# Part of the output projection made inside attention's last steps, and the first row pairs normalized two pairs later

## The chip, the cores and the metric

The kernel runs on one core of a Trainium2 chip. The metric is device time in microseconds, the median of several runs; one further execution was profiled. Engines are named as in the profile: PE (TensorE, PEld its weight loads), ACT (ScalarE), DVE (VectorE), POOL (GpSimd), SP (SyncE, which issues DMAs).

## What is computed

Four residual sublayers over x of 2048 rows and 640 columns, in float32: attention with 32 heads of 20 dimensions, then a Fourier mixing, and both again.

```python
x = x + _A_ref(_layernorm(x), A_wqkv, A_wo)        # softmax attention, o @ wo at its end
x = x + _B_ref(_layernorm(x), dft_seq..., dft_hid...)   # Real(DFT_seq(DFT_hidden(x)))
x = x + _A_ref(_layernorm(x), A_wqkv, A_wo)
x = x + _B_ref(_layernorm(x), dft_seq..., dft_hid...)
```

## The kernel before

The kernel makes two layers, each of attention and Fourier, with the same code. Matrix products other than scores and values are done with each operand split into a high and a low part (`split`, three matmuls for each product: `three`). Nothing is scheduled by a planner: the order of a Python program is the order of each engine's queue, and each engine takes its queue strictly in order.

**Attention.** `sweep` goes through 512 steps (8 groups of four heads, 4 blocks of 512 query columns, 16 blocks of 128 keys `kc`). A step n has two halves of scores, `scores(n, 0)` and `scores(n, 1)`, each two matmuls into one PSUM tile `psc` and one exp on ACT over 128 x 1024 into a tile `e`; and later `values(n)`, four matmuls of 32 columns from those two e tiles into `acc` (eight matmul records each). The tiles go round in rings:

```python
p = bank(f"p{(2 * n + j) % 3}", [128, 2, 512], "psc")
e = s.e[n, j] = s.room(f"e{(2 * n + j) % 7}", [2, 512], F32, "e")
```

so a score waits until the exp three halves back has read its tile, and an exp waits until the values that read its tile, seven halves back, are done. The values lag the scores: without filling work, a round of the loop is "s s v", where v is that of two steps before. At the end of 16 key blocks `finish` (DVE) normalizes `acc` and POOL stores the result to DRAM in 16 DMAs (`o`).

The order in a step can be written out by hand: `plan(n)` may return a string for several steps, with "s" a half of scores, "v" the values of the next owed step, "f" a call of `block` (work for PE from elsewhere) and "n" a call of `fill`. It does so in the earlier part of attention, where the rest of the QKV projection is made; there the strings are "sssfsssvvssvv" and "ssfsssvvsssvvsssfssvvsssnvv". In the last 90 steps or so there is no such work left, and the order is "ssv" throughout. In those steps DVE checks the Fourier matrices (tile `cq`), splits the weights `wo` and `wh`, and SP loads them, from a list that `done()` returns; one item of it is taken at every second step (`tasks`), not in steps 54 to 63 of 64.

**Projection** (class `Project`). The 2048 rows are 16 row tiles n, in 8 pairs p; the result of a pair is added to the pair's x (tile `xr`, four in rotation) by `product(n)`: for each half of 320 columns, 5 chunks of 128 dimensions by three matmuls, 15 in all, into one of four PSUM banks in rotation, and one DVE instruction that adds it to x with the row sums. The operand `o` comes by `fetch(k, m)` from DRAM, in tiles of two row tiles, four in rotation; two are fetched in the last steps of attention (`early`), two at the start of the projection, the others after pairs 1 and 3. After each pair:

- `normal(p - 1)`, first half: ACT scales (tile `na`), DVE combines (tile `fold`); for pairs 2, 3, 6 and 7 also DVE sums `fold2`, and in its second half ACT and DVE split them into `xn`, which the Fourier part needs;
- `moments(p)`: SP stores x, POOL makes the mean, ACT the sums of squares (`xsq`), POOL the factors (`ars`, `nb`), DVE the sums and differences `g`; for pairs 0 and 2 `edge` (ACT, DVE) handles row 0; for pair 2 DVE waits there for ACT;
- `ahead`: loads or splits parts of the Fourier matrix (tiles `craw`, `chl`).

`mids`, at the start, clears a tile on POOL and splits a few columns on ACT and DVE.

**Fourier** accumulates over the `xn` and `chl` tiles (`pacc`) and then makes the hidden transform (`phid`).

Of the kernel before, what the change touches and what calls it, by code (L numbers as in the profile page):

```python
# [19 lines left out]
ND = D // 128  # L20
# [4 lines left out]
NP = NT // 2  # L25
NQ = NT // 4
LATE = (1, 4, 6)
FIRST = (0, 1, 4, 5)
HD = D // 2
TOL = 2.0 ** -32  # L30
# [5 lines left out]
def mha_fnet_kernel(ctx, tc, x_in, wqk, wv, wo, seq, hid, nat_seq, nat_hid, out):  # L36
# [44 lines left out]
    def split(hl_h, hl_l, src, vector=False):  # L81

        if vector:
            V.tensor_copy(hl_h, src)  # L84
        else:
            A.activation(hl_h, src, AF.Copy)
        V.tensor_tensor(hl_l, src, hl_h.bitcast(F32), op=OP.subtract)  # L87

    def three(out_ap, pairs_h, pairs_l, start, stop):

        (ah, al), (bh, bl) = pairs_h, pairs_l
        PE.matmul(out_ap, ah, bh, start=start, stop=False)  # L92
        PE.matmul(out_ap, ah, bl, start=False, stop=False)  # L93
        PE.matmul(out_ap, al, bh, start=False, stop=stop)  # L94
# [37 lines left out]
    class Qkv:  # L132
# [48 lines left out]
        def fetch(s, c, room=None, tag="wraw", wait=False):  # L181
            s.raw[c] = (room or s.fill)(tag, [ND, 128], F32, "wraw")
            if wait:
                V.memset(s.raw[c][:, 0, 0:1], 0.0)
            nc.sync.dma_start(s.raw[c], wqk[c])
# [268 lines left out]
    class Attention:  # L454
# [156 lines left out]
        def run(s, done, project, check):  # L611

            work, tasks, later = s.a.work(), s.a.vweights(1, s.a.fill, pause=[lambda: None] * 2), list(check)
            s.work, s.blocks, s.after, s.rest, s.more, s.landed = True, 0, None, 0, False, 0


            def due(n):
                return s.blocks < 58 or s.blocks >= 91 or (n - 1) % NT in (2, 7, 12)

            def block(n):  # L620
                try:
                    f = next(work)
                    s.blocks += 1
                    s.more = f is True
                    s.after = (n + (2 if n < s.THIN else 4), f) if f and not s.more else None
                    s.rest = s.after[0] + 2 if s.after else n
                except StopIteration:
                    s.work = False
                    tasks.extend(done())

            def fill(n):
                if s.after:
                    if n >= s.after[0]:
                        f, s.after = s.after[1], None
                        f()
                elif s.work and n >= max(s.rest, s.THIN) and due(n + 1):
                    block(n)
                    s.rest = max(s.rest, n + 2)
                    return s.work and not s.a.silent

            def plan(n):
                if s.blocks >= 58 or s.after:
                    return
                whole = 32 <= s.blocks < 48
                if n % 4 == 1 and n + (4 if whole else 8) < s.THIN and (whole or s.blocks % 2 == 0):
                    return "sssfsssvvssvv" if whole else "ssfsssvvsssvvsssfssvvsssnvv"

            def compare(n):


                if n < 8:
                    return
                for _ in range(2):
                    if not later or n < s.landed or (len(check) - len(later)) * 490 >= n * len(check):
                        break
                    task = later.pop(0)
                    if isinstance(task, tuple):
                        s.landed = n + 5
                        task = task[1]
                    task()  # L660

            def need(n, *keys):
                while not all(k in s.a.made for k in keys):
                    if s.after:
                        fill(s.after[0])
                    else:
                        block(n)

            def begin(n, g, qb, kc):


                if qb == NB - 1 and g + 1 < H // 4:
                    when, to = 0, g + 1
                    c0, c1 = to * 80 // 128, ((to + 1) * 80 - 1) // 128
                    keys = [c0, (c1, 0) if to in LATE else c1, ND + c0, ND + c1] + (["v"] if to >= 4 else [])
                else:
                    when, to, keys = 5, g, [(((g + 1) * 80 - 1) // 128, qb + 1)]
                if to != g or g in LATE and qb < NB - 1:
                    if kc == when:
                        need(n, *keys)  # L680
                        s.shift = s.a.bound(to, s.room)
                    if kc - when in (0, 3, 5):
                        next(s.shift)

                if tasks and n % 2 == 0 and n >= 16 and n % 64 < 54:
                    tasks.pop(0)()
                for f in project.early.get(n, []):
                    f()

            s.sweep("b", begin, fill, plan, block, compare)  # L690
            assert not s.work and not later and not tasks, (len(later), len(tasks))

        def general(s, done, project):

# [231 lines left out]
    class Project:  # L926
        def __init__(s, att, src, dst):
            s.att, s.src, s.dst, s.w, s.raw = att, src, dst, {}, {}
            s.sum = {}
            s.oh, s.x, s.xn, s.rs, s.f, s.g, s.nb = {}, {}, {}, {}, {}, {}, {}  # L930

            s.early = {474: [lambda: s.fetch(0, 0)], 503: [lambda: s.fetch(0, 1)]}

        def weights(s, dc):

# [5 lines left out]
            return load, lambda: split(s.w[dc][:, 0], s.w[dc][:, 1], s.raw[dc], vector=True)  # L941

        def setup(s):
            s.ot = [s.late(f"o{m}", [2, ND, 256], F32R, "o") for m in range(2)]

        def fetch(s, k, m):

            o = s.ot[(2 * k + m) % 4]
            t = 2 * k + m * NP
            nc.sync.dma_start(o.bitcast(F32), s.att.o.rearrange("j (c p) t -> p j c t", p=128)[:, :, :, t * 128:(t + 2) * 128])  # L950
            for i in range(2):
                s.oh[4 * k + 2 * i + m] = o[:, :, :, i * 128:(i + 1) * 128]

        def load(s, p):
            if p < NP:
# [3 lines left out]
        def product(s, n):  # L959
            x = s.x[n // 2][:, n % 2]  # L960
            for i in range(2):
                p = bank(f"b{4 + (2 * n + i) % 4}", [128, 512], "py")[:, :HD]
                cols = slice(i * HD, (i + 1) * HD)
                for dc in range(ND):
                    three(p, [s.oh[n][:, k, dc] for k in range(2)],
                          [s.w[dc][:, k, cols] for k in range(2)], dc == 0, dc == ND - 1)
                V.scalar_tensor_tensor(x[:, cols], p, 1.0, x[:, cols], op0=OP.mult, op1=OP.add,  # L967
                                       accum_out=s.sums(n // 2)[:, i, n % 2:n % 2 + 1])

# [59 lines left out]
                split(xn[:, 0], xn[:, 1], t[k])  # L1029

        def run(s):
            for m in range(2):
                s.ot.append(s.room(f"o{2 + m}", [2, ND, 256], F32R, "o"))
                s.fetch(1, m)
            s.next.mids()
            for p in range(NP):
                if p:
                    s.load(p + 3)
                for n in (2 * p, 2 * p + 1):
                    s.product(n)  # L1040
                if p in (1, 3):
                    for m in range(2):
                        s.fetch(p // 2 + 2, m)

                parts = s.normal(p - 1) if p else iter(())
                next(parts, None)
                s.moments(p)
                list(parts)
                if p == 1:
                    s.next.ahead(0)  # L1050
                elif p in (3, 4, 5):
                    s.next.ahead(p - 2)
            list(s.normal(NP - 1))
# [7 lines left out]
    class Fourier:  # L1061
# [60 lines left out]

        def mids(s):
            x = s.keep("mids", [4, 80], F32R, "mids")
            G.memset(x.bitcast(F32), 0.0)
            s.mid, s.uc = [x[:, 0], x[:, 1]], [x[:, 2], x[:, 3]]
            split(s.mid[0][:, :8], s.mid[1][:, :8], s.midraw.rearrange("p r k i -> p (r k i)"))


        ORDER = (0, 1, 4, 5, 2, 6, 3, 7) + tuple(range(8, 16))  # L1130
# [250 lines left out]
    def layer(start, src, dst, general, tasks, after):  # L1381
# [14 lines left out]
        def done():  # L1396

            fill.close()
            xt.close()
            f.late = Pool(f"late{tag}", "right")  # L1400
            p.late = Pool(f"early{tag}", "right")
            pairs = [p.weights(k) for k in range(ND)] + [f.weights(k) for k in range(6)]
            out = [pairs[0][0]]
            for (_, parts), after in zip(pairs, pairs[1:] + [None]):
                out += [after[0], parts] if after else [parts]
            p.setup()
            out += [lambda: f.edges(0)] + [lambda k=k: p.load(k) for k in range(4)] + [lambda: f.edges(1)]
            return out

        if general:  # L1410
# [138 lines left out]
```

## Time and profile before

| | us |
|---|---|
| median of 3 runs (2474.61 to 2474.91) | 2474.65 |
| profiled execution | 2476.03 |
| its span (first to last instruction) | 2474.0 |
| ACT busy in it, of which exps (L521) | 2116.6, 1917.6 |
| attention's exps of the first layer, from 87.4 to the last one's end at | 1098.8 |
| projection of the first layer (tile py), starts of its matmuls from 1099.9 to | 1171.3 |

The granted clock of PE was 0.999 of full speed. In the timelines a row is: start, duration (from the first start to the last end, where several instructions are merged), engine, line, operation, tiles written <- read, shapes, count, and in brackets the idle time before it with what ended it. In the windows a row is: the window, its length, then for each engine shown its busy time and number of instructions, the granted clock, the DMA share and GB/s. An exp's record begins when ACT takes it up, so that in a gapless row of exps the records overlap. Ends of matmuls are modelled, and a busy PE is not a full one: two or four matmuls on different rows or columns of the array run side by side.

### The profile page before, as it was taken

Reading aid. Unit: us, or ns where it says so; the run is one execution under the profiler, and the core shown is the slowest. Engines: PE = TensorE matmul, PEld = TensorE weight load, DVE = VectorE, ACT = ScalarE, POOL = GpSimd, SP = SyncE. Lnnn points to the kernel's source line nnn. Section 1 sums busy time; section 2 is a strip of 40 time slices with the busy share of each in tenths; the row PEclk is TensorE's granted clock in tenths of the full one; section 3 lists DMA queues with packets and bytes.
Section 4 is the critical chain, followed back from the end, with each engine's and each line's share of the span. In section 5 each row is a group of like instructions: output and inputs, shape, how many; then the busy total and the mean of one; then the engine's idle time right before and its main releaser. Section 6 shows DMA issues by size and latency. Waiting matters only on the chain. (4 is left out here: it accounts for less than half of the span.)

```text
span 2474.0 us, 43743 instructions
## 1 busy us (share of the span) xinstructions
PE 2447.5 (99%) x16350; PEld 1174.9 (47%) x16350; DVE 984.4 (40%) x2174; ACT 2116.6 (86%) x2430; POOL 526.9 (21%) x1034
## 2 busy tenths in 40 slices
PE   8999999999999999999999999999999999999998
PEld 7644444543333332249885444454433333322596
DVE  6244442233343333416763444323333232332275
ACT  6699998899999999975457989888999999999752
POOL 2012211022111212113321212211211212222233
PEclk9999999999999999999999999999999999999999
DMA  5223231223232314427552332312221312233455
GB/s 184 99 88 125 83 110 55 75 69 118 67 100 83 107 62 130 126 86 245 190 182 95 112 100 92 109 53 70 86 77 56 96 59 72 64 97 96 130 204 194
DMA packets 127460, 262.65 MB, mean 106 GB/s; under 512 B 29168, under 2 KB 53520, under 8 KB 127236
## 3 DMA queue, kind: packets, MB, share of 16 engines
q1 hardware_dynamic: 88644, 159.88, 19.6%
q0 software_dynamic: 38592, 99.85, 12.6%
q8 instruction: 132, 2.16, 0.4%
q14 instruction: 92, 0.75, 0.1%
HBM read 175.29 MB, written 84.31 MB: 105 GB/s over the span
## 5 line engine op out<-in xcount | busy, mean ns | idle before, releaser
L521 ACT ACTIVATE e<-psc 128x1024 f32<-128x1024 f32 x2048 | 1917.6, 1120 | 105.6 <-PE psc L518 94.6
L529 PE MATMUL acc<-e,v 128*32 128x512 f32 x8192 | 1041.6, 601 | 0.4 <-DVE of L536 0.3
L518 PE MATMUL psc<-stq,stk 62*128 62x512 f32 x4096 | 765.4, 450 | 2.1 <-ACT e L521 1.1
L518 PEld LDWEIGHTS psc<-stq,stk 62*128 62x128 f32 x4096 | 340.2, 184 | 744.7 <-ACT e L521 623.6
L529 PEld LDWEIGHTS acc<-e,v 128*32 128x32 f32 x8192 | 212.2, 108 | 380.0 <-issue 344.8
L99 PE MATMUL pqk<-xt,wqk 128*128 128x512 f32 x1200 | 319.3, 407 | 0.8 <-DVE xt L87 0.6
L550 POOL DMA_DIRECT2D o<-oh x256 | 132.1, 524 | 821.0 <-DVE oh L545 809.3
L84 DVE CAST hl<-pqk 128x512 fp32r<-128x512 f32 x64 | 44.3, 692 | 599.4 <-PE pqk L99 599.4
L99 PEld LDWEIGHTS pqk<-xt,wqk 128*128 128x128 f32 x1200 | 213.1, 188 | 84.5 <-issue 39.8
L536 DVE STREAM_TRANSPOSE of<-acc 128x512 f32<-128x512 f32 x64 | 45.8, 716 | 321.0 <-PE acc L529 321.0
L99 PE MATMUL pv<-wv,xt 128*128 128x320 f32 x960 | 151.3, 313 | 0.0
L99 PEld LDWEIGHTS pv<-wv,xt 128*128 128x128 f32 x960 | 141.0, 188 | 15.5 <-issue 9.7
L550 POOL DMA_DIRECT2D o<-ot x256 | 128.7, 510 | 1.4 <-issue 1.2
L207 POOL DMA_DIRECT2D scrq<-hl x40 | 28.3, 708 | 430.2 <-DVE hl L87 240.1
L207 POOL DMA_DIRECT2D scrk<-hl x40 | 27.8, 695 | 389.6 <-DVE hl L87 280.8
L213 DVE TENSOR_REDUCE top<-pn 32x1 f32<-32x512 f32 x80 | 53.5, 676 | 121.5 <-PE pn L212 121.1
L785 DVE TENSOR_REDUCE far<-cq 128x1 f32<-128x512 f32 (+5 forms) x169 | 98.6, 584 | 5.7
L92 PE MATMUL py<-wo,o 128*128 128x320 f32 x320 | 99.2, 310 | 1.5 <-DVE xr L967 1.5
L93 PE MATMUL py<-wo,o 128*128 128x320 f32 x320 | 98.6, 308 | 0.0
L94 PE MATMUL py<-wo,o 128*128 128x320 f32 x320 | 98.6, 308 | 0.0
L789 DVE TENSOR_TENSOR cq<-cq 128x512 f32<-128x512 f32 (+4 forms) x166 | 96.4, 581 | 2.4 <-DMA cq<-in_nat_seq_dram 2.4
L243 DVE COPY v<-pv 128x320 f32<-128x320 f32 x32 | 15.7, 490 | 161.3 <-PE pv L99 161.3
(200 smaller groups left out, 1737.2 us busy)
## 6 DMA issues: line engine op xcount, KB each, us to landing
cq<-in_nat_seq_dram POOLq DMA_DIRECT2D x64, 512.0 KB, 5.2
scrq<-hl POOLq DMA_DIRECT2D x40, 512.0 KB, 3.2
scrk<-hl POOLq DMA_DIRECT2D x40, 512.0 KB, 3.1
stq<-scrq SPq DMA_DIRECT2D x256, 80.0 KB
stk<-scrk SPq DMA_DIRECT2D x128, 160.0 KB
o<-o SPq DMA_DIRECT2D x16, 1280.0 KB
stq<-scrq SPq DMA_DIRECT2D x256, 40.0 KB
stk<-scrk SPq DMA_DIRECT2D x128, 80.0 KB
```

The costliest lines, as they stand in the source:

```text
L92: PE.matmul(out_ap, ah, bh, start=start, stop=False)
L93: PE.matmul(out_ap, ah, bl, start=False, stop=False)
L94: PE.matmul(out_ap, al, bh, start=False, stop=stop)
L99: yield lambda i=i, j=j, k=k: PE.matmul(out_ap, a[i], b[j], start=dc == 0 and k == 0, stop=dc == ND - 1 and k == 2)
L207: G.dma_start(s.scr["qk"[k]][c * 128:(c + 1) * 128, :, tb * 512:(tb + 1) * 512], hl.bitcast(F32))
L213: V.tensor_reduce(s.top[:H, c // ND, c % ND, tb:tb + 1], p, op=OP.max, axis=AX.X)
L518: PE.matmul(p[:, i], s.k[g, kc // 8, j][r, kc % 8 * 128:(kc % 8 + 1) * 128], s.q[g, qb, j][r], start=True, stop=True)
L521: A.activation(e, p, AF.Exp, scale=SCALE)
L529: PE.matmul(s.acc[32 * j:32 * j + 32], s.a.v[kc][:, v0:v0 + 32], s.e[n, j // 2][:, j % 2], start=kc == 0, stop=kc == NT - 1, skip_group_ch ...
L550: G.dma_start(s.o[k, h * DH:(h + 1) * DH, qb * 512:(qb + 1) * 512], hl[k][32 * j:32 * j + DH])
L785: V.tensor_reduce(to, x, op=OP.max, axis=AX.X, apply_absolute_value=True)
L789: V.tensor_tensor(y, x, y, op=op)
```

## The change

1. `wo`'s first three chunks (DONE = 3) of row tiles 0 to 3 are made within attention's last 64 steps. `parts` is a list of eight: tiles 0 to 3 by two halves, each nine matmuls of 128x320 into the bank "fill" and one DVE add to x. From step 448 on, at every eighth step, `plan` returns one string for eight steps with one "f" in it, and `block` takes the next part.
2. `fetch` is divided: the first three chunks of an o tile and the other two are tiles of their own, each fetched by two DMAs. The first three chunks of tiles 0 and 1 (from head groups that are long finished), and the x of pairs 0 and 1, are loaded among the early items of the `done()` list; those of tile 2 at step 486.
3. `product` of row tiles 0 to 3 goes on from chunk 3: six matmuls for each half and not 15.
4. `LAG`: after pair p the pairs normalized are none (p = 0, 1), 0 (p = 2), 1 (p = 3), 2 and 3 (p = 4); from 5 on p - 1 as before.
5. `mids` is made after pair 2 and on DVE alone.

```diff
+DONE = 3
+LAG = {0: [], 1: [], 2: [0], 3: [1], 4: [2, 3]}
...
             def block(n):
+                if not s.work:
+                    project.parts.pop(0)()
+                    return
...
             def plan(n):
+                if project.parts and not s.work and n >= 448 and n % 8 == 0:
+                    return "sssfssvssvsvssvssvssvssvv"
...
-            s.early = {474: [lambda: s.fetch(0, 0)], 503: [lambda: s.fetch(0, 1)]}
+            s.begun, s.parts = set(), [lambda n=n, i=i: s.begin(n, i) for n in (0, 1, 2, 3) for i in range(2)]
+            s.early = {474: [lambda: s.fetch(0, 0, 1)], 486: [lambda: s.fetch(1, 0, 0)], 503: [lambda: s.fetch(0, 1, 1)]}
...
+        def begin(s, n, i):
+
+            p = bank("fill", [128, HD], "py")
+            cols = slice(i * HD, (i + 1) * HD)
+            for dc in range(DONE):
+                three(p, *s.operands(n, dc, cols), dc == 0, dc == DONE - 1)
+            x = s.x[n // 2][:, n % 2, cols]
+            V.tensor_tensor(x, p, x, op=OP.add)
+            s.begun.add(n)
...
+                first = DONE if n in s.begun else 0
+                for dc in range(first, ND):
+                    three(p, *s.operands(n, dc, cols), dc == first, dc == ND - 1)
...
-            for m in range(2):
-                s.ot.append(s.room(f"o{2 + m}", [2, ND, 256], F32R, "o"))
-                s.fetch(1, m)
-            s.next.mids()
+            s.ot[2] += s.heads(s.room, 2, (1,))
+            s.ot.append(s.heads(s.room, 3))
+            for m, part in ((0, 1), (1, 0), (1, 1)):
+                s.fetch(1, m, part)
...
-                parts = s.normal(p - 1) if p else iter(())
-                next(parts, None)
+                parts = iter(())
+                for k in LAG.get(p, [p - 1]):
+                    list(parts)
+                    parts = s.normal(k)
+                    next(parts, None)
                 s.moments(p)
                 list(parts)
                 if p == 1:
                     s.next.ahead(0)
+                elif p == 2:
+                    s.next.mids()
...
-            G.memset(x.bitcast(F32), 0.0)
+            V.memset(x.bitcast(F32), 0.0)
...
+            for k, m in ((1, 0), (3, 1)):
+                along(k, lambda m=m: p.fetch(0, m, 0))
+            for k, m in ((5, 0), (6, 1)):
+                along(k, lambda m=m: p.load(m))
```

More of the change, by code (lines that the diff above doesn't have):

```diff
@@ L690, in run @@
             s.sweep("b", begin, fill, plan, block, compare)
-            assert not s.work and not later and not tasks, (len(later), len(tasks))
+            assert not s.work and not later and not tasks and not project.parts, (len(later), len(tasks))
         def general(s, done, project):
@@ L943, in setup, with heads, fetch, operands @@
         def setup(s):
-            s.ot = [s.late(f"o{m}", [2, ND, 256], F32R, "o") for m in range(2)]
-        def fetch(s, k, m):
-            o = s.ot[(2 * k + m) % 4]
+            s.ot = [s.heads(s.late, m) for m in range(2)] + [s.heads(s.late, 2, (0,))]
+        @staticmethod
+        def heads(room, m, parts=(0, 1)):
+            return [room(f"o{m}{'ab'[k]}", [2, (DONE, ND - DONE)[k], 256], F32R, "o") for k in parts]
+        def fetch(s, k, m, part):
+            o = s.ot[(2 * k + m) % 4][part]
             t = 2 * k + m * NP
-            nc.sync.dma_start(o.bitcast(F32), s.att.o.rearrange("j (c p) t -> p j c t", p=128)[:, :, :, t * 128:(t + 2) * 128])
+            dims = slice(DONE, ND) if part else slice(DONE)
+            src = s.att.o.rearrange("j (c p) t -> p j c t", p=128)[:, :, dims, t * 128:(t + 2) * 128]
+            for j in range(2):
+                nc.sync.dma_start(o[:, j].bitcast(F32), src[:, j])
             for i in range(2):
-                s.oh[4 * k + 2 * i + m] = o[:, :, :, i * 128:(i + 1) * 128]
+                s.oh[4 * k + 2 * i + m, part] = o[:, :, :, i * 128:(i + 1) * 128]
+        def operands(s, n, dc, cols):
+            o, c = (s.oh[n, 0], dc) if dc < DONE else (s.oh[n, 1], dc - DONE)
+            return [o[:, k, c] for k in range(2)], [s.w[dc][:, k, cols] for k in range(2)]
+        def begin(s, n, i):
[6 more added lines that the diff above has]
+            s.begun.add(n)
         def load(s, p):
@@ L963, in product @@
                 cols = slice(i * HD, (i + 1) * HD)
-                for dc in range(ND):
-                    three(p, [s.oh[n][:, k, dc] for k in range(2)],
-                          [s.w[dc][:, k, cols] for k in range(2)], dc == 0, dc == ND - 1)
+                first = DONE if n in s.begun else 0
+                for dc in range(first, ND):
+                    three(p, *s.operands(n, dc, cols), dc == first, dc == ND - 1)
                 V.scalar_tensor_tensor(x[:, cols], p, 1.0, x[:, cols], op0=OP.mult, op1=OP.add,
@@ L1042, in run @@
                     for m in range(2):
-                        s.fetch(p // 2 + 2, m)
-                parts = s.normal(p - 1) if p else iter(())
-                next(parts, None)
+                        for part in range(2):
+                            s.fetch(p // 2 + 2, m, part)
+                parts = iter(())
[3 more added lines that the diff above has]
+                    next(parts, None)
                 s.moments(p)
@@ L1124, in mids @@
             x = s.keep("mids", [4, 80], F32R, "mids")
-            G.memset(x.bitcast(F32), 0.0)
+            V.memset(x.bitcast(F32), 0.0)
             s.mid, s.uc = [x[:, 0], x[:, 1]], [x[:, 2], x[:, 3]]
-            split(s.mid[0][:, :8], s.mid[1][:, :8], s.midraw.rearrange("p r k i -> p (r k i)"))
+            split(s.mid[0][:, :8], s.mid[1][:, :8], s.midraw.rearrange("p r k i -> p (r k i)"), vector=True)
         ORDER = (0, 1, 4, 5, 2, 6, 3, 7) + tuple(range(8, 16))
@@ L1406, in done, with along @@
             p.setup()
-            out += [lambda: f.edges(0)] + [lambda k=k: p.load(k) for k in range(4)] + [lambda: f.edges(1)]
+            def along(k, *fs):
+                first = out[k]
+                out[k] = lambda: [f() for f in (first, *fs)]
+            for k, m in ((1, 0), (3, 1)):
+                along(k, lambda m=m: p.fetch(0, m, 0))
+            for k, m in ((5, 0), (6, 1)):
+                along(k, lambda m=m: p.load(m))
+            out += [lambda: f.edges(0)] + [lambda k=k: p.load(k) for k in (2, 3)] + [lambda: f.edges(1)]
             return out
```

## The prediction

> **What bounds the kernel now.** I read the page's engine table first, then its groups, then the attention in windows, then the timeline of its last steps. Two rows of the page name the pair that matters:
>
> ```profile
> PE 2447.5 (99%) x16350; PEld 1174.9 (47%) x16350; DVE 984.4 (40%) x2174; ACT 2116.6 (86%) x2430; POOL 526.9 (21%) x1034
> L521 ACT ACTIVATE e<-psc 128x1024 f32<-128x1024 f32 x2048 | 1917.6, 1120 | 105.6 <-PE psc L518 94.6
> ```
>
> PE at 99% says little, since its records overlap. The exps (L521) are 1917.6 of the span's 2474.0 us, so the question for the last 64 steps of attention, where the change puts PE work, is whether ACT or PE ends last there. The windows of the exps, one before that stage and one in it:
>
> ```profile
> 864.00:920.00 56.00, 55.34 (x60) 1.00 0.23 72
> 985.00:1095.00 110.00, 110.00 (x122) 1.00 0.29 90
> ```
>
> In the stage ACT has no gap at all: it binds. The timeline of a step there, and the layer's last exps:
>
> ```profile
> 991.17 0.19 PEld L518 LDWEIGHTS psc<-stq,stk 62*128 62x128 f32 x2 [0.84 <-ACT e L521]
> 991.17 0.91 PE L518 MATMUL psc<-stq,stk 62*128 62x512 f32 x4
> 991.58 0.19 PEld L518 LDWEIGHTS psc<-stq,stk 62*128 62x128 f32 x2 [0.22 <-ACT e L521]
> 992.01 1.06 PE L529 MATMUL acc<-e,v 128*32 128x512 f32 x8
> 993.01 0.91 PE L518 MATMUL psc<-stq,stk 62*128 62x512 f32 x4
> ...
> 1077.12 21.72 ACT L521 ACTIVATE e<-psc 128x1024 f32<-128x1024 f32 x23
> 1097.39 1.46 ACT L521 ACTIVATE e<-psc 128x1024 f32<-128x1024 f32 x1
> ```
>
> From first to last start, 22 exps take 20.27 us: 0.92 each. A step is 1.84 us (991.17 to 993.01), and the second score pair waits for an exp. What would PE need, left alone? Earlier, where it is loaded with projection blocks:
>
> ```profile
> 372.02 0.96 PE L518 MATMUL psc<-stq,stk 62*128 62x512 f32 x6
> 372.92 2.47 PE L99 MATMUL pv<-wv,xt 128*128 128x320 f32 x15
> 375.32 0.97 PE L518 MATMUL psc<-stq,stk 62*128 62x512 f32 x6
> ...
> 372.62 2.86 ACT L521 ACTIVATE e<-psc 128x1024 f32<-128x1024 f32 x3 [0.55 <-PE psc L518]
> ...
> 703.28 0.73 PE L518 MATMUL psc<-stq,stk 62*128 62x512 f32 x4
> 703.94 1.07 PE L529 MATMUL acc<-e,v 128*32 128x512 f32 x8
> 704.94 0.73 PE L518 MATMUL psc<-stq,stk 62*128 62x512 f32 x4
> 705.60 1.92 PE L529 MATMUL acc<-e,v 128*32 128x512 f32 x16
> 707.46 0.73 PE L518 MATMUL psc<-stq,stk 62*128 62x512 f32 x4
> ```
>
> By starts: "ss" 0.66, "sss" 0.90 (so a lone "s" 0.42), "v" 1.00, "vv" 1.86 us. Score start to exp start is 0.60 and the exp then lasts 1.02; since a score record lasts about 0.5, the hop is 0.1. A step costs PE 1.66 against ACT's 1.84: 1.4 us spare in eight steps.
>
> **Part 1: what leaves the projection.** Of each of the first four row tiles, 3 of 5 chunks go: 2 x 9 matmuls, 72 per layer.
>
> ```profile
> 1101.00:1135.00 34.00, 34.00 (x234) 33.95 (x233) 5.71 (x24) 1.00 0.89 304
> 1135.00:1138.00 3.00, 2.26 (x16) 2.00 (x15) 1.71 (x8) 1.00 0.12 44
> 1138.00:1171.00 33.00, 33.00 (x228) 33.00 (x227) 6.93 (x30) 1.00 0.68 232
> ```
>
> These are windows of tile py (PE, PEld, DVE). 67.0 us for 462 matmuls is 0.145 each, PE without a hole but for 0.7 us in the middle window. Removed: 72 x 0.145 = 10.4 us per layer. The Trainium skill (TensorE: Matmul & The Clock Gate, Back-to-back issue gap) gives the isolated gap as N/2.4 + 2.5 ns, 136 ns for 320 columns; by it 9.8 us would go. The row decides, as weight loads fill PEld as fully as PE here.
>
> **Part 2: what the attention gets.** A block F is 9 such matmuls: the block of 15 took 2.40 (372.92 to 375.32), less 6 x 0.145: 1.53 us (bounds 1.4 to 1.7). A cycle is then, on PE alone, sss 0.90 + F 1.53 + six ss 3.96 + s 0.42 + six v 6.00 + vv 1.86 = 14.67 us; ACT needs 16 x 0.92 = 14.72. By throughput it fits exactly. But it must also fit the rings: scores() has 3 PSUM tiles and 7 e tiles, so exp t waits until the values of exp t-7 are done, and score t until exp t-3 is. At step 448 the sweep owes two steps of values, so the cycle's first v is that of step n-2, and it stands behind sss, F and ss. The fourth exp (e3) writes the tile this v reads. I walk one cycle from its first score, in us:
>
> - s0 0, s1 0.34, s2 0.57, F 0.90, s3 2.43, s4 2.76; exps e0 to e2 end at 1.62, 2.54, 3.46.
> - First v 3.09 to 4.16 (its record is 1.07). e3 could have run by 3.46; it starts at 4.26 and ends at 5.28 instead of 4.38. e4 ends 6.20.
> - s5 4.09. s6 needs e3's PSUM tile: not at 4.42 but 5.33, wait 0.91. Second v 5.66 to 6.73; e5 writes a tile it reads: ends 7.85 instead of 7.12. e6 ends 8.77.
> - s7 6.66, third v 7.08, s8 8.08; s9 needs e6: 8.82 instead of 8.41, wait 0.41. The next three pairs wait 0.18 each, ACT being then the slower.
> - So PE takes 14.67 + 0.91 + 0.41 + 0.54 = 16.53 and the next cycle begins there. Against 14.72: +1.81, x 8 = +14.5 us per layer (13 to 16 with F 1.4 to 1.7).
>
> In the trace of before no exp waits for a v, so this wait is read from the code alone; its length comes from the rows above. The eight adds on DVE (0.49 each by the py rows below) cost nothing: DVE has two thirds of the stage free, and the "fill" bank is wanted again only a cycle later.
>
> ```profile
> 1000.00:1050.00 50.00, 49.98 (x330) 14.56 (x326) 17.54 (x40) 50.00 (x56) 9.19 (x17) 1.00 0.42 136
> ```
>  The third weight chunk is split at 963.90 (next fence), some 16 us before step 448 (its first exp stands 127 x 0.92 before the last at 1097.39, at 980.6). Were that late, the first F would wait and hold every score behind it. SP's queue has the q loads behind the early fetches; they are asked for 12 steps ahead of use (kc 4 of 16).
>
> **Part 3: the projection's head.** PE gets to pairs 2 and 3 sooner; POOL, ACT and DVE do not get their statistics sooner.
>
> ```profile
> 963.90 0.82 DVE L87 TENSOR_TENSOR wo<-woraw,wo 128x640 fp32r<-128x640 f32 x1
> ...
> 1099.88 0.42 PE L92 MATMUL py<-wo,o 128*128 128x320 f32 x1
> ...
> 1103.18 0.69 DVE L546 TENSOR_TENSOR ot<-ot,oh 128x512 f32<-128x512 f32 x1
> 1105.44 2.00 POOL L550 DMA_DIRECT2D o<-ot  x4
> 1108.18 0.49 DVE L967 SCALAR_TENSOR_TENSOR xr<-py,xr 128x320 f32<-128x320 f32 x1
> 1108.60 0.48 DVE L967 SCALAR_TENSOR_TENSOR xr<-py,xr 128x320 f32<-128x320 f32 x1
> 1110.00 0.82 POOL L982 TENSOR_TENSOR mean<-rowsum 128x2 f32<-128x2 f32 x1 [2.18 <-DVE xr L967]
> 1118.41 0.20 POOL L982 TENSOR_TENSOR mean<-rowsum 128x2 f32<-128x2 f32 x1 [0.48 <-DVE xr L967]
> 1123.69 0.21 POOL L1002 TENSOR_SCALAR nb<-ars 128x1 f32<-128x1 f32 x1
> 1127.21 0.43 POOL L982 TENSOR_TENSOR mean<-rowsum 128x2 f32<-128x2 f32 x1 [3.31 <-DVE xr L967]
> 1135.59 0.47 DVE L967 SCALAR_TENSOR_TENSOR xr<-py,xr 128x320 f32<-128x320 f32 x1
> 1137.23 0.54 DVE L1019 SCALAR_TENSOR_TENSOR fold<-g,ars,na 128x321 f32<-128x321 f32 x1
> 1139.87 0.81 DVE L996 TENSOR_TENSOR g<-xr 128x638 f32<-128x638 f32 x1
> 1144.02 0.48 DVE L967 SCALAR_TENSOR_TENSOR xr<-py,xr 128x320 f32<-128x320 f32 x1
> ...
> DMA to landing us min/median/max: 1.8/3.5/5.8
> ```
>
> Count from the first py, at 1099.88. Pair 0 is 24 matmuls, done at 3.5. DVE finishes attention's last block at 4.0 and then drains py; pair 1 needs the first bank at 4.5: stall 1.0. (The mids on POOL held that drain to 1108.18 = 8.3; moved, they no longer do.) Pair 1 ends at 8.0, pairs 2 and 3 at 8.7 each, at 25.4. The last row is tile o's: what pair 2 still fetches is issued within 2.5, lands by 8.3 even at 5.8, and is wanted at 8.0 + 9 x 0.145 = 9.3; later, it would hold PE by as much.
>
> Pair 4 needs pair 3's drain, which stands in DVE's order behind the second edge row, that of pair 2. That is the end of a serial chain over POOL and ACT: POOL free of its stores at 1107.44 = 7.6; pair 0's statistics and edge some 7.9 (1110.00 up to just before 1118.41, less the 0.48 wait); pair 1's 5 to 5.5 (1118.41 to 1123.90); pair 2's until DVE is free 8.4 (1127.21 to 1135.59). Sum 28.9 to 29.4, plus mids on DVE about 0.5 and the drain 0.4: about 30. Some of this overlaps (each pair's mean starts in the tail of the one before); I take a stall of 4.0, bounds 2 to 5.
>
> In pair 4 DVE now normalizes pairs 2 and 3. Before, one such normal with its g and two chl parts takes 6.8 (1137.23 to 1144.02); the second adds 2.64 (1137.23 to 1139.87) and 1.5 for xn: 11 to 11.5, then the drain. From pair 4's end to the bank that pair 6 wants: 0.25 + 0.4 + 11.4 + 0.45 = 12.5, under which PE has pair 5, 8.7: stall 3.8 (bounds 2 to 5). The pairs after go as before, and Fourier starts by that much earlier or later.
>
> **Sum.** Per layer -10.4 + 14.5 + (1.0 + 4.0 + 3.8 - 0.7 of before's own stall) = +12.2; two layers +24.4. The profiled execution took 2476.03 us, span 2474.0, and would take 2500.4; the median of the runs is 1.4 lower, 2474.65, and becomes 2499.0.
>
> **Rivals.** A. *The e ring does not bind, the filling is free* (faster). Had the first v ended by 3.36, e3 would lose nothing; that needs F of at most 0.73 us, half of what its matmuls take, or one owed step instead of two. For it speaks the equality 14.67 to 14.72, and the free stage of before. Then the projection's -10.4 + 8.1 = -2.3 stays, less about 1 for the tightness: 2472; with the projection's stalls also at before's 0.7, 2 x -10.4: 2454. Chance 0.09. The Trainium skill's Perfetto Trace Analysis (Optimization Strategy) says that regimes with different bounds may gain from being interleaved, which is this rival; the same page (Identifying Performance Opportunities) takes repeated bubbles on the engine that should be saturated as a sign of too few tiles, which is my forecast. No trace here shows yet which of the two holds.
>
> B. *The ring binds, but the projection keeps its saving* because the normalizing two pairs later leaves DVE ahead of PE: per layer 14.5 - 10.4 = +4.1, 2483. Against it: the one stall that before shows is just this edge chain. Chance 0.15, still slower.
>
> C. *The two cancel*: ring at 8 us per layer and projection -8: 2475. Chance 0.05. That the change is not made at all needs parts left when step 448 comes; the exps have 64 steps and the list eight parts, one to a cycle, so I give it nothing beyond C.
>
> **Numbers.** Forecast 0.71; alone it spans 2486 (ring 13, projection -7.5 per layer) to 2507 (ring 16, stalls of 11: 2 x (16 - 10.4 + 10.3)). The range goes down to 2482 so that B is in it; A and C stay out. I count a run within 0.2% (5 us) as no change, about what a measurement of this kernel can tell. Faster 0.09 (A), within 0.05 (C), slower 0.86.
>
> **What would show it.** In the last 64 steps the exps should no longer be at 0.92 without a gap: two idle spots per eight steps, ended by PE acc, and a stage of some 132 us instead of 118. In the projection the stream of py should break in pair 1, ahead of pair 4 and ahead of pair 6, on DVE xr. It is wrong if ACT stays gapless there, or if py runs through.

## The result, and the profile after

The changed kernel takes 2516.12 us (median of 6 runs) against 2474.63 us on the same chip, ratio 1.017 [1.0157, 1.0183]: 41.5 us more, where the prediction had 24.4 more (2499.0) and 2507 as the end of its range. Its profiled execution took 2519.91 us (span 2518.0), the longest of the six; what differs between the two traces outside the two places below is 1.6 us ahead of the first exp, which most of the kernels below do not show, and 2.5 us behind the second layer's projection, whose cause was not traced; the six executions differ by 4.9 us among themselves.

**Attention's last 64 steps.** Two windows of the exps in the changed kernel, in the places of the two shown before the change (length, ACT busy, count, clock, DMA share, GB/s), and the exps' row on its page (the lines L521, L529 and L518 are now L523, L531 and L520; L967 is L996):

```profile
866.00:922.00 56.00, 55.30 (x60) 1.00 0.24 74
986.00:1112.00 126.00, 112.67 (x121) 1.00 0.22 63
```

```profile
L523 ACT ACTIVATE e<-psc 128x1024 f32<-128x1024 f32 x2048 | 1922.7, 1059 | 133.4 <-PE psc L520 98.5
```

About as many exps as before now need 126 us and not 110, and ACT, which had no gap there, stands idle for 13.3 of them. From the start of step 448 to the end of the last exp the first layer takes 134.4 us (982.37 to 1116.75) instead of 118.0, the second 134.9 instead of 118.1. One cycle of eight steps in the timeline of the changed kernel, first PE, then ACT:

```profile
999.28 0.96 PE L520 MATMUL psc<-stq,stk 62*128 62x512 f32 x6
1000.17 0.41 PE L94 MATMUL py<-wo,o 128*128 128x320 f32 x1
...
1001.69 0.73 PE L520 MATMUL psc<-stq,stk 62*128 62x512 f32 x4
1002.35 1.07 PE L531 MATMUL acc<-e,v 128*32 128x512 f32 x8
1003.35 0.50 PE L520 MATMUL psc<-stq,stk 62*128 62x512 f32 x2
1004.59 0.50 PE L520 MATMUL psc<-stq,stk 62*128 62x512 f32 x2 [0.74 <-ACT e L523]
1005.02 1.07 PE L531 MATMUL acc<-e,v 128*32 128x512 f32 x8
...
999.90 2.86 ACT L523 ACTIVATE e<-psc 128x1024 f32<-128x1024 f32 x3 [0.21 <-PE psc L520]
1003.51 1.94 ACT L523 ACTIVATE e<-psc 128x1024 f32<-128x1024 f32 x2 [0.75 <-PE acc L531]
1006.18 4.69 ACT L523 ACTIVATE e<-psc 128x1024 f32<-128x1024 f32 x5 [0.73 <-PE acc L531]
```

The first v starts 3.07 us into the cycle (walked: 3.09). The fourth exp starts only after it has ended, at 4.23 (walked: 4.26), and the sixth after the second v, at 6.90 (walked: 6.83): two idle spots in every cycle, each ended by PE acc, as foretold, and a third, small one of 0.21 at the cycle's head, which the walk did not have.

**The projection.** From the first to the last start of a py matmul it takes 74.6 us in both layers, with 72 matmuls fewer than before, when it took 71.4. Windows of tile py (PE, PEld, DVE, then clock, DMA share, GB/s):

```profile
1118.00:1143.00 25.00, 24.24 (x163) 23.98 (x164) 5.45 (x24) 1.00 0.80 261
1143.00:1149.00 6.00, 1.51 (x9) 1.25 (x8) 1.13 (x5) 0.87 1.03 401
1149.00:1154.00 5.00, 5.00 (x21) 5.00 (x20) 0.60 (x4) 0.50 0.54 166
1154.00:1168.00 14.00, 14.00 (x96) 14.00 (x95) 1.99 (x8) 0.99 0.92 314
1168.00:1173.00 5.00, 1.35 (x8) 1.09 (x7) 0.98 (x5) 0.84 0.81 261
1173.00:1178.00 5.00, 5.00 (x20) 5.00 (x20) 0.75 (x4) 0.50 0.68 236
```

The second and fifth windows are the stalls ahead of pairs 4 and 6. The windows behind them, the third and the last, are what the forecast had not priced: PE is busy throughout and makes 21 and 20 matmuls in 5 us, where 0.147 us each would make 34. The granted clock is 0.50. What DVE does in the two stalls, from its timeline:

```profile
1144.53 0.48 DVE L1151 TENSOR_TENSOR c3raw<-c3raw,ea 1x321 f32<-1x321 f32 x1 [5.57 <-ACT ea L1038]
...
1147.18 0.33 DVE L1160 MEMSET mids<- 128x320 f32 x1
...
1147.87 0.49 DVE L996 SCALAR_TENSOR_TENSOR xr<-py,xr 128x320 f32<-128x320 f32 x1
...
1160.58 0.55 DVE L1048 SCALAR_TENSOR_TENSOR fold<-g,ars,na 128x321 f32<-128x321 f32 x1
...
1165.15 0.55 DVE L1048 SCALAR_TENSOR_TENSOR fold<-g,ars,na 128x321 f32<-128x321 f32 x1 [0.21 <-ACT na L1038]
...
1167.88 0.81 DVE L1025 TENSOR_TENSOR g<-xr 128x638 f32<-128x638 f32 x1
...
1170.82 1.28 DVE L89 TENSOR_TENSOR chl<-craw,chl 128x512 fp32r<-128x512 f32 x2
1172.02 0.48 DVE L996 SCALAR_TENSOR_TENSOR xr<-py,xr 128x320 f32<-128x320 f32 x1
```

Ahead of pair 4 it stands 5.57 us idle for ScalarE's part of the second edge row, then makes that row and the mids, and drains the banks (L996) last, at 1147.87. Ahead of pair 6 it is busy with the two normals of pair 4, from 1160.58 to 1172.02, with one gap of 0.21. Those are the two causes the prediction gave.

The stalls, as the distance from one py start to the next less 0.147, were 0.88, 4.65 and 3.81 us in the first layer, 0.88, 4.45 and 3.82 in the second. Behind each long one 20 to 22 matmuls are 0.267 us apart and not 0.147: 2.3 to 2.6 us lost each time, some 4.9 us per layer.

### The profile page after: what moved, and what is told of

It is laid out like the page before. It is cut to its first block, busy times and chain, and to the rows that moved or that the text cites. A ratio compares the mean times of both kernels' runs of the same rounds, so it can differ in the third digit from the quotient of the medians.

```text
span 2518.0 us, 43834 instructions
## 1 busy us (share of the span) xinstructions
PE 2455.8 (98%) x16350; PEld 1186.9 (47%) x16350; DVE 993.5 (39%) x2194; ACT 2120.7 (84%) x2428; POOL 522.4 (21%) x1032
## 5 line engine op out<-in xcount | busy, mean ns | idle before, releaser
L523 ACT ACTIVATE e<-psc 128x1024 f32<-128x1024 f32 x2048 | 1922.7, 1059 | 133.4 <-PE psc L520 98.5
L531 PE MATMUL acc<-e,v 128*32 128x512 f32 x8192 | 1037.1, 600 | 3.9 <-DVE of L538 3.9
L520 PE MATMUL psc<-stq,stk 62*128 62x512 f32 x4096 | 760.6, 448 | 16.3 <-ACT e L523 15.3
L520 PEld LDWEIGHTS psc<-stq,stk 62*128 62x128 f32 x4096 | 338.6, 184 | 744.8 <-ACT e L523 619.9
L531 PEld LDWEIGHTS acc<-e,v 128*32 128x32 f32 x8192 | 213.7, 108 | 388.6 <-issue 351.4
L94 PE MATMUL py<-wo,o 128*128 128x320 f32 x320 | 106.1, 332 | 17.5 <-DVE xr L996 17.5
L95 PE MATMUL py<-wo,o 128*128 128x320 f32 x320 | 103.2, 323 | 0.0
L96 PE MATMUL py<-wo,o 128*128 128x320 f32 x320 | 103.0, 322 | 0.0
```

Of the source, the lines that this page charges most:

```text
L520: PE.matmul(p[:, i], s.k[g, kc // 8, j][r, kc % 8 * 128:(kc % 8 + 1) * 128], s.q[g, qb, j][r], start=True, stop=True)
L523: A.activation(e, p, AF.Exp, scale=SCALE)
L531: PE.matmul(s.acc[32 * j:32 * j + 32], s.a.v[kc][:, v0:v0 + 32], s.e[n, j // 2][:, j % 2], start=kc == 0, stop=kc == NT - 1, skip_group_ch ...
```

## The experiments

All times are medians, beside runs of the kernel before on the same chip (2474.9 to 2475.0).

**One v moved.** The attention theory (a ring of seven exp tiles; the first v of a cycle comes too late) against TensorE's time for the blocks: one owed v is taken ahead of the first cycle, so that all later ones are a step earlier; not one instruction less.

```diff
-    return "sssfssvssvsvssvssvssvssvv"
+    return ("v" if n == 448 else "") + "sssfssvssvsvssvssvssvssvv"
```

> The changed kernel with one more v ahead of the first cycle, so that the sweep owes one step of values and not two all through the last 64 steps; same work, same order otherwise. Ring theory (an exp of the cycle waits for the first v, which stands behind the block of nine): the waits go, the stage from step 448 on falls from 134.5 to about 119.5 us in each layer, the whole to 2516.1 - 30 = 2486. Rival (the nine matmuls simply cost PE time, or the DVE add or the early fetches hold the stage): no change, 2516.

Measured 2486.85 us, ratio 1.0047 [1.003, 1.0064]: 29.3 us less than the changed kernel, for the place of one v in each layer. The windows of the exps:

```profile
985.00:1098.00 113.00, 111.57 (x122) 1.00 0.24 70
```

122 exps in 113 us. The stage takes 119.8 and 120.4 us and not 134.4 and 134.9. So attention's loss is the ring, but for the some 2 us a layer by which the stage is still longer than before the change.

**The blocks thrown away, and the blocks empty.** In the first kernel the early blocks are computed in attention and not used: the projection makes all five chunks again, and the normalizing is as before the change; DVE's adds of the blocks are left out. In the second the blocks are empty as well; in attention only the order is left.

```diff
-LAG = {0: [], 1: [], 2: [0], 3: [1], 4: [2, 3]}
+LAG = {0: []}
...
-            x = s.x[n // 2][:, n % 2, cols]        # first kernel
-            V.tensor_tensor(x, p, x, op=OP.add)
...
-                first = DONE if n in s.begun else 0
+                first = 0
```

> The blocks of nine in attention alone: they are computed as in the changed kernel but thrown away, the projection makes all its chunks and normalizes each pair one pair later as before. Ring theory: the stage at 134.5 us as in the changed kernel, the projection at 71.5 as before, so 2474.6 + 2 x 16.5 = 2508. If part of the attention's loss came from the DVE adds, less: about 2500. If the added blocks were free: 2475.

> The kernel whose early blocks were thrown away (it ran 2510.6: the whole projection is computed and normalized as before), now with those blocks empty: the last 64 steps keep their cycles of eight, but no py matmul stands in them. What attention loses there is then the order alone. By the walk of scores, values and the seven exp tiles, a cycle in the order sss, ss, v without a block still loses 13.2 us in the 64 steps, against 14.7 with the block; the block is worth 1.5 of it and the order the rest: 2510.6 - 2 x 1.5 to 2.5 = 2506 to 2508. If the loss is TensorE's time for the blocks (9 matmuls, 1.5 us in each of eight cycles, 12 us a layer), the time goes to 2475 to 2487.

Measured 2510.63 us (1.0143 [1.0126, 1.016]) and 2511.1 us (1.0146 [1.0129, 1.0163]). Without DVE's adds the stage is as long as in the changed kernel (134.40 us in the first layer, there 134.38), so they have no part in the loss. The order without a block costs nearly as much as with it: 133.75 us in the first layer. Emptying the blocks is worth 0.65 us there, where the walk had 1.5. In the second layer the empty blocks take 138.12 against 134.45: PE's clock is at 0.50 there for 6.83 us twice, from 2225.38 and from 2327.78, and the two cycles in which this happens are 2.1 us longer than their counterparts in the first layer. So the whole times can't price the block, and both sides of the second expectation missed, the rival's by far. A cycle of the kernel with empty blocks, PE and then ACT:

```profile
1014.06 0.97 PE L520 MATMUL psc<-stq,stk 62*128 62x512 f32 x6
1015.76 0.50 PE L520 MATMUL psc<-stq,stk 62*128 62x512 f32 x2 [0.74 <-ACT e L523]
1016.68 0.49 PE L520 MATMUL psc<-stq,stk 62*128 62x512 f32 x2 [0.41 <-ACT e L523]
1017.10 1.07 PE L531 MATMUL acc<-e,v 128*32 128x512 f32 x8
...
1014.69 2.85 ACT L523 ACTIVATE e<-psc 128x1024 f32<-128x1024 f32 x3 [0.22 <-PE psc L520]
1018.26 1.02 ACT L523 ACTIVATE e<-psc 128x1024 f32<-128x1024 f32 x1 [0.72 <-PE acc L531]
```

Without a block the fourth and fifth scores still wait for the exps that free their PSUM tiles, and the first v starts 3.04 us into the cycle, 0.03 sooner than with a block. The block stands in time in which PE would wait; what does the harm is five scores ahead of the first v.

**The later normalizing alone.** The changed kernel without its blocks: attention's order is "ssv" again and the projection makes all chunks. Of the change, `LAG`, the move of the mids and the divided fetches are left.

> The later normalizing alone (and mids after pair 2 on DVE): no blocks in attention, the projection makes all its chunks. If DVE's load in pair 4, where two pairs are normalized, is what stops PE ahead of pair 6, that stall of some 4 us and the slow clock behind it (2.6 us) are here too, and pair 4 waits about 1 us: projection 78, the whole 2474.6 + 2 x 6.5 = 2488. Rival (the stalls come only from the head that is too fast for POOL and ACT): the projection runs through, 2474.6.

Measured 2491.07 us, ratio 1.0065 [1.0048, 1.0082]: 16.2 us more than before, with attention's stage as long as before (117.9 us). Stalls of 1.85 and 3.82 us in the first layer (1.66 and 3.82 in the second) and 13 and 19 matmuls at half rate behind the longer one.

**The slow stream: dummies, twice.** If PE's standing still makes the half rate, work in the stall should remove it. The first kernel put 28 and 22 matmuls ahead of pairs 4 and 6, each of them started and stopped; the second 26 and 21 as one chain.

```diff
+    for k in range(fill):
-        PE.matmul(idle, ..., start=True, stop=True)
+        PE.matmul(idle, ..., start=k == 0, stop=k == fill - 1)
```

> The changed kernel with matmuls whose result nobody reads ahead of row pairs 4 and 6 of the projection: 28 before pair 4 (4.1 us) and 22 before pair 6 (3.2 us), less than PE stands idle there (4.6 and 3.8 us). Clock theory (after an idle stretch PE is granted half its clock for some us, which costs about 2.6 us after each of the two stalls): the granted clock stays at 1.00, the projection falls from 74.6 to about 69.5 us, the whole by 2 x 5.2 to 2506. Rival (the matmuls after the stall are slow because the DMA engines are full in these windows, share 1.0): no gain, 2516, or worse by what the added matmuls delay.

> The changed kernel with 26 and 21 extra matmuls, one accumulating chain each whose result nobody reads, ahead of pairs 4 and 6, where TensorE stands still for 4.8 and 4.0 us. In the earlier kernel with such matmuls each of them started and ended a sum of its own in one bank; they came 0.47 us apart, not 0.147, and the granted clock fell to 0.50 all the same. In a chain they should come 0.147 apart and take 3.8 and 3.1 us, inside the standing time. If the slow stream behind the two stalls (267 ns from py to py instead of 147, some 20 to 22 matmuls each, 2.4 to 2.6 us) is a clock that falls because TensorE stands still, the two windows stay near clock 1.0 and the time is 2516.1 - 2 x 5.0 = 2506. If it comes from the DMAs that run at the same time, or from work that the stalled engines catch up on, the stream stays slow and the time stays 2516 or rises by up to 1.

The first ran 2557.25 us (1.0333 [1.0316, 1.035]), 41 us more than the changed kernel. The clock theory had 2506; the rival had room for it, as what the added matmuls delay. Its windows of PE, and then the group of the first 28 dummies:

```profile
1145.00:1150.00 5.00, 4.47 (x10) 0.79 0.96 352
1150.00:1155.00 5.00, 4.59 (x8) 0.50 0.41 115
```

```profile
L1069 PE MATMUL idle<-wo,o 128*128 128x320 f32 x28 | 15.0, 534 | 1.6
```

Each dummy began 0.06 us after the record of the one before had ended: 0.47 us apart, and the clock fell to 0.50 though an instruction was on PE nearly always; 0.69 apart from then on. They took 15.0 us where the stall to fill was 4.65, so this run can't tell the theories apart. In a chain:

```profile
1141.00:1147.00 6.00, 5.29 (x36) 1.00 1.03 409
1147.00:1152.00 5.00, 5.00 (x37) 1.00 0.53 158
```

The clock stays at 1.00, with the DMA share as high as before (1.03); 2506.61 us (1.0127 [1.0109, 1.0145]) where 2506 was expected. The stalls are as long as ever (4.69 and 3.82 from py to py in the first layer), and 9.5 us are gone: the half rate was the price of standing still, not of the DMAs.

**The two stalls, one repair each.** Pairs normalized without a double (2 in pair 4, 3 in pair 5; 4 and 5, which have no partner, both in pair 6); and, apart from that, the order of normalizing from before.

```diff
-LAG = {0: [], 1: [], 2: [0], 3: [1], 4: [2, 3]}
+LAG = {0: [], 1: [], 2: [0], 3: [1], 4: [2], 5: [3], 6: [4, 5]}     # first kernel
+LAG = {0: []}                                                      # second kernel
```

> The changed kernel, but pairs 2 and 3 aren't normalized both in pair 4: 2 goes in pair 4, 3 in pair 5, and 4 and 5, which have no partner to be folded with and cost VectorE 1.1 us each, both in pair 6. If the stall ahead of pair 6 is VectorE's second normalizing in pair 4, it and the slow clock behind it go: 2516.1 - 2 x (3.9 + 2.5) = 2503. If the stall only passes on to the pair with the two that follow, with some 2 us of it left and without a slow clock, 2508; if VectorE has no slack at all from there on, 2516.

> The changed kernel with the order of normalizing from before (each pair one pair later); the early blocks stay. By the theory that the stall ahead of pair 4 is the serial chain of the first three pairs' statistics and of the second edge row over ScalarE and GpSimd, that stall stays, split or not, 4 to 5 us with or without its slow clock, and the one ahead of pair 6 goes: 2503 to 2508. If the later normalizing is what feeds the first pairs (VectorE waiting in order for ScalarE's scaled rows would hold the drains of pairs 1 to 3), the stalls move into pairs 2 and 3 and the time is 2512 to 2518.

Measured 2502.75 us (1.0109 [1.0091, 1.0127]; expected 2503) and 2498.66 us (1.0095 [1.0077, 1.0113]; expected 2503 to 2508). In the first, the stall ahead of pair 6 and its slow clock are gone and the one ahead of pair 4 is there in full. In the second the waiting is spread (0.88, 1.64 and 2.76 us), and little or nothing runs at half rate behind it (9 matmuls in one layer, none in the other). In the change as it was made, the later normalizing cost 17.5 us.

**Three repairs at once.** The v ahead, the spread order, and DVE's part of the second edge row taken after pair 3's drains.

```diff
-            if not first:
-                V.tensor_tensor(e[:, :HD + 1], ...)   # and what follows
+            if first:
+                return
+            def rest():
+                V.tensor_tensor(e[:, :HD + 1], ...)   # the same
+            s.rest = rest
...
+                if p == 3:
+                    s.next.rest()                     # after both products of pair 3
                 parts = iter(())
```

> Three repairs at once: one v block taken ahead of the first cycle of eight (as in the kernel that ran 2486.9), pairs normalized as spread over pairs 4, 5 and 6, and VectorE's part of the second edge row (two additions, the split and its two copies) taken after pair 3's products instead of before its drains. By the theory that attention loses by its seven exp tiles alone and the projection by these two stalls and their slow clock: projection 408 x 0.147 + 1.0 = 61 us instead of 71.6 and 73.8, so 2486.9 - 10.6 - 12.8 = 2463.5. If the chain over ScalarE and GpSimd itself is longer than TensorE's work in the first four pairs, whatever waits for it, stalls of some 5 us a layer stay: 2474. If the Fourier transform behind it can't start earlier, 2487.

Measured 2460.35 us, ratio 0.9943 [0.9925, 0.9961]: 55.8 us less than the changed kernel and 14.6 less than the kernel before. Its py, in the windows that hold the first two pairs' stall, the place ahead of pair 4, and the rest:

```profile
1102.00:1127.00 25.00, 24.24 (x163) 23.97 (x164) 6.87 (x30) 1.00 0.77 246
1127.00:1133.00 6.00, 6.00 (x43) 6.00 (x42) 0.50 (x2) 1.00 1.03 409
1133.00:1163.00 30.00, 30.00 (x206) 29.87 (x204) 6.75 (x30) 1.00 0.84 290
```

One stall of 0.84 is left, and in the second layer one of 0.68; the projection takes 60.7 and 61.5 us, attention's stage 119.8. Alone, the v was worth 29.3 us and the spread 13.4; 13.1 remain for the edge row. That was not tried alone, but against the kernel with only the spread order the two projections are 12.9 us shorter in sum (67.5 and 67.7 there).

**Another order, and the old normalizing, in that kernel.**

```diff
-    return ("v" if n == 448 else "") + "sssfssvssvsvssvssvssvssvv"
+    return "ssvssvssvsvssvssvssfsssvv"          # first kernel
-LAG = {0: [], 1: [], 2: [0], 3: [1], 4: [2], 5: [3], 6: [4, 5]}
+LAG = {0: []}                                  # second kernel
```

> The kernel with the three repairs (2460.35), but the v block ahead of the first cycle is given up and the cycle itself is put in another order: ssv ssv ssv sv ssv ssv ss, block, sssvv. The walk has every v in it early enough for the exp seven tiles later, and loses 1.3 us in the 64 steps where the one with the v ahead loses 1.5; the 0.8 us that the v ahead costs in the 32 steps before it goes too: 2458 to 2460. If a block beside five scores holds ScalarE whatever the values do, it loses as the changed kernel does, 16 us a layer: 2489.

> The kernel with the three repairs (2460.35), but every pair is normalized one pair later, as before the change. In the changed kernel with that order the stalls were 0.9 in pair 1, 1.6 ahead of pair 3 and 2.8 ahead of pair 4. If the later normalizing is of use with early blocks, the one of 1.6 stays and the one ahead of pair 4, which was the second edge row's, goes: 2460.4 + 2 x 1.6 to 2 = 2464. If the postponed edge row alone is what counts, 2460; if pair 3's own normalizing then stands where the edge row stood, 2466 to 2470.

Measured 2461.32 us (0.9945 [0.9928, 0.9961]) and 2470.01 us (0.9981 [0.9971, 0.9991]). The first order needs no v ahead: here too a block stands beside five scores, with the v's early enough for the ring, and the stage takes 120.9 us, 2.9 more than before the change (walked: 1.3). No difference to the kernel above can be told. The time of the second is that of the third case, at the upper end of its 2466 to 2470: stalls of 1.6 us ahead of pair 3 and 1.97 ahead of pair 5. From the edge row's part to pair 4's first drain DVE takes 9.6 us (1130.23 to 1139.84) where the kernel above takes 6.8 (1128.56 to 1135.40), since the normal between them has sums and a split. Behind the 1.97 the clock falls too (PE busy, clock, DMA share, GB/s):

```profile
1137.20:1140.61 3.41, 1.60 (x11) 1.00 0.90 311
1140.62:1144.02 3.40, 3.40 (x14) 0.50 1.01 328
```

So normalizing later is right with the early blocks, and worth 9.7 us, once pairs 2 and 3 are no longer both normalized in one pair and the edge row is out of the way.

## Why the prediction was off, step by step

- **Which side, and the ring: right.** Slower was forecast with 0.86. The places of the first and second v and of the two idle exps were met within 0.08 us, and one moved v took all but some 2 us of the loss away.
- **The ring's size: +14.5 forecast, +16.4 and +16.8 measured**, beyond the upper bound of 16. A cycle takes about 16.7 us and not 16.53 (the 0.21 at its head), the first one 17.5, the one before the change 14.68 and not 14.72.
- **"That needs F of at most 0.73 us": wrong.** Rival A's condition let the block decide when the first v starts. With the block empty the first layer still loses 15.8 us (with it 16.4), since the scores ahead of that v wait for their PSUM tiles. The other half of the condition, one owed step and not two, is what the moved v did.
- **The removed matmuls: right.** 72 x 0.147 is 10.6; the forecast took 10.4.
- **The stalls: right.** 1.0 + 4.0 + 3.8 were forecast; 0.88 + 4.65 + 3.81 came, at the three places and from the causes named.
- **The step that failed: the sum of the projection,** -10.4 + 8.1 = -2.3 per layer. It let PE go on at 0.145 us a matmul the moment a stall ended, so that the slow clock behind a stall stood in the sum as nothing. Per layer the traces give -10.6 + 8.4 + 4.9 for the half rate, 2.7 in all, and the stage grew by 3.2. That is 2 x 5.5 us of the 17 missed, the ring's size 2 x 2.1, and 0.3 a layer lies between the last exp and the first py; some 1.3 us of the medians' difference is assigned to nothing.
- **B and "the stall is just this edge chain": half right.** Of the two long stalls the edge row makes only one: with the doubled normals repaired alone, the one ahead of pair 4 is there in full (4.67). The edge row was not repaired alone.

On the half rate the Trainium skill has a rule which the forecast did not weigh: TensorE: Matmul & The Clock Gate, Part 1 (The HAM clock gate), says that the clock goes to half after about an idle window of 3.4 us, that this window runs freely, and that about as much sustained work brings it back. The rows agree on the half (0.50) and, as shown below, on a window that no program sets. They differ on the length: 1.97 us of standing still was enough.

| stall ahead of PE, us | stalls in these kernels | with a half rate behind, matmuls |
|---|---|---|
| 4.45 to 4.68, nothing in it | 6 | 6, 15 to 22 |
| 3.81 to 3.82, nothing in it | 6 | 5, 13 to 20 |
| 2.75 to 2.76 | 2 | 1, 9 |
| 1.97 | 2 | 2, 12 and 14 |
| up to 1.85 | all others | none |

The table alone doesn't say why 1.97 sets it off in both layers and 2.76 in only one; the clock in the traces does. In the changed kernel the stretches at 0.50 behind stalls begin at 1147.47, 1171.37, 2393.34 and 2417.23 us. The later three are 7, 365 and 372 times 3.413 us behind the first, and each lasts 6.83, twice 3.413: the clock changes on a fixed grid, while PE still stands or already runs (PE busy, clock, DMA share, GB/s):

```profile
1147.40:1147.47 0.07, 0.00 (x0) 1.00 1.52 432
1147.48:1154.29 6.81, 5.87 (x22) 0.50 0.67 219
```

In every other kernel with several such stretches their starts lie on a grid of 3.413 us too. So the part of a stall that falls into one cell of the grid is what matters. These are the cells of the three doubtful cases: the 2.76 of the old order in the first layer and the 2.75 in its second, and the 3.82 without a half rate, which is in the first layer of the kernel with the moved v:

```profile
1142.68:1146.09 3.41, 1.38 (x10) 1.00 1.01 406
```

```profile
2378.30:2381.72 3.42, 2.46 (x17) 1.00 1.03 389
2381.72:2385.13 3.41, 1.78 (x12) 1.00 0.96 320
```

```profile
1151.66:1155.07 3.41, 1.53 (x11) 1.00 0.60 138
1155.07:1158.49 3.42, 1.64 (x11) 1.00 0.95 307
```

The first leaves 2.03 us of one cell empty, and the clock falls; the second is split into 0.96 and 1.63, the third into 1.88 and 1.78, and it holds. The 1.97 above lies whole in one cell (1.81 empty by PE's records, as their ends are modelled). All other stalls with a half rate behind them empty at least 2.0 us of a cell, all others without one at most 1.5. For py the boundary is thus near 1.8 to 1.9 us of 3.41; 1.81 with a fall against 1.88 without one is as fine as these records can tell.

The other rule that the forecast cited, in Perfetto Trace Analysis, takes repeated gaps on the engine that should be saturated as a possible sign of too few tiles. The gaps were these, and the tiles were seven; but the kernels with a v ahead and with the other order closed them, but for 1.4 to 2.0 us a layer, without one tile more.

## What to carry to other kernels

Work put into a stage that another engine binds may be free, and yet the order written to make room for it is not: ask of each instruction in the new order which buffer it frees, and walk the ring, with the block empty too. When a change takes work off one engine, price a stall twice: its length, and the slow clock behind it; several short waits cost less here than one long one. And where a term is postponed, look where it lands: two normals in one pair cost more than the wait they removed, and one instruction that waits in a strict queue (here the edge row) is better put behind the drains that other engines need.

## What the runs showed of the hardware

Within a projection that runs for 70 us, TensorE's granted clock falls to 0.50 after stalls of 2 to 4.7 us. It falls and comes back on a grid of 3.413 us, for one cell (3.41 us) or two (6.83), part of which can still lie in the stall; a matmul then comes every 0.267 us and not every 0.147. A stall of 3.82 us that the grid divides evenly did nothing, one of 1.97 within one cell did.

An instruction on PE is not enough to hold the clock: started and stopped singly in one bank, the same matmul came every 0.47 us and the clock fell; as one accumulating chain it came every 0.147 and the clock held at 1.00. In the attention with empty blocks it fell twice behind cells of which PE's records fill 2.34 and 2.26 of 3.41 us, while other cells there, filled no more, had no such effect; what decides in that stream stays open. So it does for one fall in the last Fourier part of each of the two kernels with one stall repaired (2451.87 and 2446.57 us).
